# Last weight pair staged as two halves in shared float tiles, in place of four quarters in small ones

## The chip, the cores and the metric

The kernel runs on one core of one Trainium2 chip. The metric is device time in microseconds (us) of one execution; lower is better. The core has TensorE (PE) for matmuls, with its weight loads shown as a row of their own (PEld), VectorE (DVE), ScalarE (ACT), GpSimd (POOL), and SyncE (SP), which here issues all the transfers. Each engine takes its instructions strictly in the order in which the program holds them, and waits for other engines through semaphores.

## The reference, cut to what matters

An attention over 8 batches and 8 heads (576 positions, 64 dims) adds a downsampled softmax attention and a local one (distance under 4); its output is 4,608 tokens of 512 features, which go through a two-matrix feed-forward with a squared ReLU.

```
def _attn_ref(q, k, v):
    q_d = q.reshape(B, H, Sd, factor, D).mean(axis=3)   # k_d, v_d alike, factor 4
    out_up = np.repeat(sm_attn(q_d, k_d, v_d), factor, axis=2)
    mask = np.abs(pos[:, None] - pos[None, :]) < factor
    scores = np.where(mask, scale * np.matmul(q, k.transpose(0, 1, 3, 2)), -1000000000.0)
    ...
    return (out_up + np.matmul(attn, v)).astype(np.float32)

def _moe_ref(x, w_in, w_out, s, b):
    h = x @ w_in                  # (4608, 512) @ (512, 2048)
    r = np.maximum(h, 0.0)
    g = s * (r * r) + b
    return (g @ w_out).astype(np.float32)
```

The weights arrive as 64-bit floats (read as pairs of 32-bit integers), so each must be converted before use.

## The kernel before

**Feed-forward.** Tokens are worked in 18 tiles of 256 (index t), the 2,048 hidden features in 8 pairs of 128 (index p). One step (t, p) is `gemm1`, 24 matmuls of 256 columns into `ph`, then ACT's ReLU, square and cast (`gh`) and DVE's remainder (`gl`), and two or three steps later `gemm2`, 12 matmuls of 512 columns into `po`. The list `order` sets the steps: t = 0 and 1 alternate over p = 0 to 6 (steps 0 to 13), t = 2 over p = 0 to 6 (steps 14 to 20), then p = 7 for t = 0, 1, 2 (steps 21 to 23), then t = 3 onwards with all eight p.

**Weights.** `split_w(p)` makes the weights of pair p, `wi` and `wo`, as a high part (a cast on ACT) and a low part (a subtraction on DVE). `convert` does it for one chunk in seven instructions: ACT scales the top words into a float tile `es` (L226), DVE clips, shifts and twice merges bits (L227 to L230), ACT casts (L231), DVE subtracts (L234). Pairs 0 to 6 are staged whole, 1,024 columns of 64-bit words, in memory that later pairs will occupy (`STAGE`), in chunks of `CHUNK[p]` columns. The last pair, p = 7, has no such memory left: it comes in four quarters of 256 columns for each of its two matrices (`load_quarter`), in tiles with the tag `pv`, of which there are two; the quarter's `es` takes the other one. So the next quarter can be loaded only when the one before has been converted.

**Shared memory.** The single tiles `os` and `xl2` (4 KB in each partition) serve as `es` for pairs 2 to 6, then as token tile t = 2 (`split_x(2)` writes `xh` into `os` and `xl` into `xl2`), and later for outputs.

**Attention between the steps.** `advance` lets the attention of later batches go forward between the steps. `first_unit(b, hp)` is one unit: downsampled scores `sa`, local scores `sl` for the first and the second head (48 matmul records each), softmax on ACT and DVE, transposes `tp` and `tr`, then `up` and two products `ol`. Its PSUM banks come from a ring:

```
rings = {1: banks(5, 6), 2: banks(5), 3: banks(2, 3, 5)}
yield from first_unit(*units[i], rings[min(i // HP + i // (EU - 2), 3)])
```

Units (2, 0) and (2, 1) have bank 5 alone: each of their PSUM results must be read by DVE or ACT before the next can be written.

**Bias rows.** After step 13 `add_rows` sums the rows of all `wo` into `bias`, p = 7 first: 31 DVE additions of 512 columns (L577, L579), wanted only at step 21.

**What decides the order.** A scheduler puts every engine's instructions in order at build time, by priorities and a timeline of its own; the source order alone does not tell it.

Of the kernel before, what the change touches and what calls it, by code (L numbers as in the profile page):

```python
# [13 lines left out]
I32 = mybir.dt.int32  # L14
# [5 lines left out]
P = 128  # L20
# [28 lines left out]

STAGE = (6, 6, 7, 6, 7, 6, 7)  # L50
CONVERT_AT = (1, 2, 4, 6, 7, 8, 11)
CHUNK = (512, 512, 512, 1024, 1024, 512, 1024)
BEHIND = {1: 400, 2: 100, 4: 100, 5: 400}
HF = 7
GROUPS = [(i // HP, i % HP // 2) for i in range(EU, B * HP, 2)]
# [7 lines left out]
def attention_ffn_kernel(ctx, tc, qk, vw_in, vr_in, vdm, qkn, vn, w_in, w_out, s_in, b_in, out):  # L63
    nc = tc.nc
# [3 lines left out]
    one = ctx.enter_context(tc.tile_pool(name="one", bufs=1))  # L68
    two = ctx.enter_context(tc.tile_pool(name="two", bufs=2))
# [122 lines left out]
    wi, wo, wst = {}, {}, {}  # L192

    src_i = w_in.bitcast(I32).rearrange("(k c) f -> c k f", c=P)
    src_o = w_out.bitcast(I32).rearrange("(j f) c -> f j c", f=P)
# [6 lines left out]
            nc.sync.dma_start(st.rearrange("p (k f) t -> p k (f t)", k=src.shape[1]), src)  # L202
            wst[(p, op)] = st

    def load_quarter(p, op, i):
        if op == "i":
            src = src_i[:, i, 512 * p : 512 * p + 512]
        else:
            src = src_o[:, 2 * p + i // 2, 512 * (i % 2) : 512 * (i % 2) + 512]
        st = two.tile([P, 256, 2], I32, tag="pv", name="wst")  # L210
        nc.sync.dma_start(st.rearrange("p f t -> p (f t)"), src)
        return st

    def convert(st, hi, lo, op, p):


        n = hi.shape[1]
        top, low = st[:, :, 1], st[:, :, 0]
        if p in (0, 1, 7):
            f = two.tile([P, n], F32, tag="pv", name="es")  # L220
        else:
            f = one.tile([P, n], F32, tag="xl2" if op == "i" else "os", name="es")
        w = f.bitcast(I32)


        nc.scalar.mul(f, top.bitcast(F32), 2.0 ** -112)  # L226
        nc.vector.tensor_scalar(f, f, W_MAX, -W_MAX, ALU.min, ALU.max)  # L227
        nc.vector.tensor_scalar(w, w, 3, 0x7FFFFFF8, ALU.logical_shift_left, ALU.bitwise_and)
        nc.vector.scalar_tensor_tensor(w, low, 29, w, ALU.logical_shift_right, ALU.bitwise_or)
        nc.vector.scalar_tensor_tensor(w, top, -0x80000000, w, ALU.bitwise_and, ALU.bitwise_or)  # L230
        nc.scalar.copy(hi, f)  # L231
        for i in range(0, n, 512):
            js = slice(i, min(i + 512, n))
            nc.vector.tensor_tensor(lo[:, js], f[:, js], hi.bitcast(F32)[:, js], ALU.subtract)  # L234

    def split_w(p):
        with tc.high_priority(offset=-BEHIND.get(p, 0)):
            split_parts(p)

    def split_parts(p):  # L240
        wi[p] = one.tile([P, 2, NK, 256], F32R, tag=f"wi{p}", name="wi")
        wo[p] = one.tile([P, 2, 2, DM], F32R, tag=f"wo{p}", name="wo")
        for op, w in (("i", wi[p]), ("o", wo[p])):
            fl = w.rearrange("p s k f -> p s (k f)")
            if p < len(STAGE):
                st = wst.pop((p, op))
                for j in range(0, 1024, CHUNK[p]):
                    js = slice(j, j + CHUNK[p])
                    convert(st[:, js], fl[:, 0, js], fl[:, 1, js], op, p)
            else:  # L250
                for i in range(4):
                    cs = slice(256 * i, 256 * i + 256)
                    convert(load_quarter(p, op, i), fl[:, 0, cs], fl[:, 1, cs], op, p)


    xt = {}
# [513 lines left out]
```

## Time and profile before

| | us |
|---|---|
| median of 3 runs | 974.49 (971.71 to 974.57) |
| profiled execution, its own time | 972.49 |
| its span, first to last instruction | 970.7 |
| PE busy in the span | 938.7 (97%) |
| DVE, ACT, POOL busy | 637.7, 475.0, 418.0 |

Times in the trace count from the start of the span. A matmul's recorded end is modelled, so PE's busy share says that it had work, and not how fast it went; the distance from one matmul's start to the next tells that. "Idle before" a row is the engine's idle time just ahead of it, with the instruction that ended it.

### The profile page before, as it was taken

To read this page: it belongs to the slowest core of one execution; us is meant where nothing else is said; L and a number is where in the kernel's file an instruction comes from. 1 tells how busy PE (TensorE), PEld (TensorE's weight loads), DVE (VectorE), ACT (ScalarE), POOL (GpSimd) and SP (SyncE) were. 2 spreads that over 40 slices of the span, in tenths; PEclk is the share of its full clock that TensorE was granted. 3 is DMA by queue.
4 is the path that set the end of the run, shared out by engine and by line. 5 is a ranking of instruction groups with operands and counts; after the bars stand their busy time and mean duration, and the time that the engine had idled before them with its cause. 6 is when DMAs were issued, how large, how long until landed. Compare 5 with 4: busy or idle time off the path is not lost.

```text
span 970.7 us, 18541 instructions
## 1 busy us (share of the span) xinstructions
PE 938.7 (97%) x7316; PEld 843.4 (87%) x7316; DVE 637.7 (66%) x1175; ACT 475.0 (49%) x1141; POOL 418.0 (43%) x455
## 2 busy tenths in 40 slices
PE   5769999999999999999999999999999999999998
PEld 4559988888999999998888899989899999998987
DVE  5999996864567878787787878787878521211121
ACT  5878775553754453545363545453635433333231
POOL 9421011101066686776868786867676200000000
PEclk9999999999999999999999999999999999999999
DMA  9736512112243232323241424242412000000000
GB/s 316 261 121 210 172 60 78 49 42 73 101 134 113 77 110 72 102 70 133 67 136 66 135 68 131 72 134 69 136 55 76 1 22 1 23 1 22 1 23 22
DMA packets 32103, 86.26 MB, mean 89 GB/s; under 512 B 3344, under 2 KB 7952, under 8 KB 32016
## 3 DMA queue, kind: packets, MB, share of 16 engines
q1 hardware_dynamic: 32016, 85.08, 26.6%
q8 instruction: 57, 0.93, 0.4%
q14 instruction: 30, 0.25, 0.1%
HBM read 75.63 MB, written 9.44 MB: 88 GB/s over the span
## 4 chain that ended last, share of the span: by engine, by line
PE 74%; DVE 9%; DMA 8%; POOL 5%; ACT 2%; issue 2%; SPq 0%; DVEq 0%; ACTq 0%; POOLq 0%
PE ph L556 11%; PE ph L557 11%; PE ph L558 11%; PE po L603 11%; PE po L601 11%; PE po L602 11%; DMA tqk<-in_qk_dram 3%; POOL pr L466 3%; POOL acc L488 3%; DMA wst<-in_moe_w_out_dram 2%; PE sa L303 2%; DVE bias L579 1%; PE up L339 1%; PE ol L431 1%; DMA lqk<-in_qkn_dram 1%
## 5 line engine op out<-in xcount | busy, mean ns | idle before, releaser
L556 PE MATMUL ph<-xh,wi 128*128 128x256 f32 x1152 | 325.4, 283 | 3.7 <-ACT xh L542 2.5
L557 PE MATMUL ph<-xl,wi 128*128 128x256 f32 x1152 | 323.9, 281 | 0.0
L558 PE MATMUL ph<-xh,wi 128*128 128x256 f32 x1152 | 323.6, 281 | 0.0
L466 POOL TENSOR_TENSOR pr<-lqk 128x576 f32<-128x576 f32 x140 | 201.2, 1461 | 73.2 <-DMA lqk<-in_qkn_dram 29.2
L556 PEld LDWEIGHTS ph<-xh,wi 128*128 128x128 f32 x1152 | 217.5, 189 | 11.2 <-ACT xh L542 2.8
L557 PEld LDWEIGHTS ph<-xl,wi 128*128 128x128 f32 x1152 | 217.4, 189 | 5.4 <-issue 0.2
L558 PEld LDWEIGHTS ph<-xh,wi 128*128 128x128 f32 x1152 | 217.6, 189 | 0.3
L566 ACT ACTIVATE ph<-ph 128x512 f32<-128x512 f32 x144 | 83.8, 582 | 229.0 <-PE ph L558 223.2
L601 PE MATMUL po<-wo,gh 128*128 128x512 f32 x456 | 180.7, 396 | 0.0
L602 PE MATMUL po<-wo,gh 128*128 128x512 f32 x456 | 180.5, 396 | 0.0
L603 PE MATMUL po<-wo,gl 128*128 128x512 f32 x456 | 177.9, 397 | 0.0
L569 DVE TENSOR_TENSOR gl<-ph,gh 128x512 fp32r<-128x512 f32 x114 | 77.8, 683 | 115.8 <-ACT gh L568 115.5
L488 POOL TENSOR_TENSOR acc<-acc,pv 128x576 f32<-128x576 f32 x80 | 114.4, 1430 | 57.1 <-DVE acc L488 29.5
L468 DVE TENSOR_REDUCE st<-pr 128x9 f32<-128x576 f32 x140 | 105.9, 757 | 37.7 <-POOL pr L466 35.4
L292 POOL TENSOR_TENSOR dq<-vq 64x64 f32<-64x64 f32 x58 | 22.8, 393 | 197.4 <-PE up L337 195.3
L603 PEld LDWEIGHTS po<-wo,gl 128*128 128x128 f32 x456 | 85.7, 188 | 17.6 <-issue 0.2
L487 DVE TENSOR_TENSOR pv<-lv,st 128x576 f32<-128x576 f32 x120 | 87.5, 747 | 18.8 <-POOL acc L488 18.4
L601 PEld LDWEIGHTS po<-wo,gh 128*128 128x128 f32 x456 | 85.7, 188 | 15.9 <-ACT gh L568 0.6
L602 PEld LDWEIGHTS po<-wo,gh 128*128 128x128 f32 x456 | 85.7, 188 | 15.8
L568 ACT CAST gh<-ph 128x512 fp32r<-128x512 f32 x114 | 66.9, 587 | 64.3 <-PE po L602 62.4
L567 ACT ACTIVATE ph<-ph 128x512 f32<-128x512 f32 x144 | 83.7, 582 | 3.2
L602 PE MATMUL po<-wo,gb 128*128 128x512 f32 x120 | 47.1, 392 | 0.0
(149 smaller groups left out, 1239.3 us busy)
## 6 DMA issues: line engine op xcount, KB each, us to landing
tqk<-in_qk_dram SPq DMA_DIRECT2D x30, 584.0 KB, 4.1
lqk<-in_qkn_dram SPq DMA_DIRECT2D x20, 768.0 KB, 4.2
lv<-in_vn_dram SPq DMA_DIRECT2D x20, 480.0 KB, 3.4
out_dram<-os SPq DMA_DIRECT2D x17, 512.0 KB, 3.1
wst<-in_moe_w_in_dram SPq DMA_DIRECT2D x7, 1024.0 KB, 6.5
wst<-in_moe_w_out_dram SPq DMA_DIRECT2D x7, 1024.0 KB, 5.3
tvd<-in_vdm_dram SPq DMA_DIRECT2D x29, 160.0 KB, 2.9
tvr<-in_vr_dram SPq DMA_DIRECT2D x29, 128.0 KB, 3.1
```

What stands on the lines that cost most here:

```text
L466: nc.gpsimd.tensor_tensor(pr, lqk[:, 0:CH], lqk[:, CH + o : 2 * CH + o], ALU.mult)
L468: nc.vector.tensor_reduce(ls[:, :, o], pr, AX.X, ALU.add)
L487: nc.vector.tensor_tensor(pv, lv[:, o : o + CH], w, ALU.mult)
L488: (nc.vector if o % 3 == 1 else nc.gpsimd).tensor_tensor(acc[:, :, h], acc[:, :, h], pv, ALU.add)
L556: nc.tensor.matmul(ph[:, j], wi[p][:, 0, k, f], xh[:, k], start=(k == 0), stop=False)
L557: nc.tensor.matmul(ph[:, j], wi[p][:, 0, k, f], xl[:, k], start=False, stop=False)
L558: nc.tensor.matmul(ph[:, j], wi[p][:, 1, k, f], xh[:, k], start=False, stop=(k == NK - 1))
L566: nc.scalar.activation(ph, ph, AF.Relu)
L567: nc.scalar.activation(ph, ph, AF.Square)
L601: nc.tensor.matmul(po[m], gh[:, j, ms], wo[p][:, 0, j], start=first, stop=False)
L602: nc.tensor.matmul(po[m], gh[:, j, ms], wo[p][:, 1, j], start=False, stop=False)
L603: nc.tensor.matmul(po[m], gl[:, j, ms], wo[p][:, 0, j], start=False, stop=last)
```

## The change

The p = 7 weights come in two halves of 512 columns for each matrix, the first staged in `os` and the second in `xl2`, so two halves of a matrix can be in flight at once; the second matrix's halves need the same two tiles. The float tile `es` of p = 6 moves from `os` and `xl2` to the two `pv` tiles (2 KB), and so p = 6 is converted in chunks of 512 columns in place of 1,024. There are 4 loads of 512 KB in place of 8 of 256 KB, and 4 conversions in place of 8 for p = 7, 4 in place of 2 for p = 6.

```
-CHUNK = (512, 512, 512, 1024, 1024, 512, 1024)
+CHUNK = (512, 512, 512, 1024, 1024, 512, 512)
...
-    def load_quarter(p, op, i):
-        if op == "i":
-            src = src_i[:, i, 512 * p : 512 * p + 512]
-        else:
-            src = src_o[:, 2 * p + i // 2, 512 * (i % 2) : 512 * (i % 2) + 512]
-        st = two.tile([P, 256, 2], I32, tag="pv", name="wst")
-        nc.sync.dma_start(st.rearrange("p f t -> p (f t)"), src)
+    def load_half(p, op, i):
+
+        src = src_i[:, 2 * i : 2 * i + 2, 512 * p : 512 * p + 512] if op == "i" else src_o[:, 2 * p + i]
+        st = one.tile([P, 512, 2], I32, tag=("os", "xl2")[i], name="wst")
+        to = st.rearrange("p (k f) t -> p k (f t)", k=2) if op == "i" else st.rearrange("p f t -> p (f t)")
+        nc.sync.dma_start(to, src)
         return st
...
-        if p in (0, 1, 7):
+        if p in (0, 1, 6, 7):
             f = two.tile([P, n], F32, tag="pv", name="es")
...
-                for i in range(4):
-                    cs = slice(256 * i, 256 * i + 256)
-                    convert(load_quarter(p, op, i), fl[:, 0, cs], fl[:, 1, cs], op, p)
+                for i in range(2):
+                    cs = slice(512 * i, 512 * i + 512)
+                    convert(load_half(p, op, i), fl[:, 0, cs], fl[:, 1, cs], op, p)
```

The scheduler then orders three engines and SP's queue anew from step 0 to step 24; POOL's order stays as it was, and behind step 27 PE's does too. From the changed function on, the changed kernel's line numbers are one lower, so L578 there is L579 here.

SP's queue, where it issues the last quarters; before:

```order
L211 DMA wst<-in_moe_w_in_dram 128x512 x2
L114 DMA tvr<-in_vr_dram 128x256
L114 DMA tvd<-in_vdm_dram 80x512
L211 DMA wst<-in_moe_w_out_dram 128x512
L114 DMA tvw<-in_vw_dram 128x768
L211 DMA wst<-in_moe_w_out_dram 128x512 x3
L114 DMA tqk<-in_qk_dram 128x1168
```

And with the change:

```order
L210 DMA wst<-in_moe_w_in_dram 128x2x512 x2
L114 DMA tvw<-in_vw_dram 128x768
L210 DMA wst<-in_moe_w_out_dram 128x1024 x2
L114 DMA tqk<-in_qk_dram 128x1168
L114 DMA tvr<-in_vr_dram 128x256
```

The halves stand next to each other in two pairs, and one attention load (`tqk`) stands right behind the second pair. Two more quarters (of `wi`) stood further ahead in the queue before; they are gone.

DVE's queue around the first local scores `sl` of unit (2, 0), the unit with bank 5 alone, at steps 14 and 15; before, the last quarter's conversion (`es`, `wo`) stands ahead of them and among them, and the bias rows begin behind them:

```order
L230 SCALAR_TENSOR_TENSOR es<-wst,es 128x256
L393 TENSOR_REDUCE sm<-sl 128x6
L234 TENSOR_TENSOR wo<-es,wo 128x256
L394 TENSOR_TENSOR pl<-sl,sm 128x192
L577 TENSOR_TENSOR bias<-wo 128x512
L569 TENSOR_TENSOR gl<-ph,gh 128x512
```

And with the change, from the last product `ol` of the unit before, (1, 3), up to the same two readings of `sl` (here L392 and L393):

```order
L433 TENSOR_TENSOR x<-ol,ups 128x288
L578 TENSOR_TENSOR bias<-bias,wo 128x512
L542 TENSOR_TENSOR xl<-x,xh 128x4x192
L578 TENSOR_TENSOR bias<-bias,wo 128x512 x2
L303 TENSOR_REDUCE dmx<-sa 96x3
L277 TENSOR_REDUCE kd<-tqk 128x144
L578 TENSOR_TENSOR bias<-bias,wo 128x512 x2
L311 RECIPROCAL dsm<-dsm 96x3
L578 TENSOR_TENSOR bias<-bias,wo 128x512
L392 TENSOR_REDUCE sm<-sl 128x6
L578 TENSOR_TENSOR bias<-bias,wo 128x512
L393 TENSOR_TENSOR pl<-sl,sm 128x192
```

All conversions now stand ahead of this stretch, and 12 of the bias additions have moved ahead of the scores' reduction; one more stands between the two readings of `sl`.

PE's queue at the same scores; before, eight matmuls of `gemm2` stand between the first head's scores (the row with x22 ends them) and the second's:

```order
L388 MATMUL sl<-tqk 32x32 x22
L603 MATMUL po<-wo,gl 128x512
L601 MATMUL po<-wo,gh 128x512
L602 MATMUL po<-wo,gh 128x512
L603 MATMUL po<-wo,gl 128x512 x2
L601 MATMUL po<-wo,gh 128x512
L602 MATMUL po<-wo,gh 128x512
L603 MATMUL po<-wo,gl 128x512
L383 LDWEIGHTS idb
L383 MATMUL sl<-maskb,idb 128x192
L388 MATMUL sl<-tqk 32x32 x24
```

And with the change, right behind the 24 matmuls of step 14:

```order
L557 MATMUL ph<-xh,wi 128x256
L382 LDWEIGHTS idb
L382 MATMUL sl<-maskb,idb 128x192
L387 MATMUL sl<-tqk 32x32 x24
L382 LDWEIGHTS idb
L382 MATMUL sl<-maskb,idb 128x192
L387 MATMUL sl<-tqk 32x32 x24
L600 MATMUL po<-wo,gh 128x512
```

The two heads' scores follow each other directly, one step earlier than before.

## Rows read from the trace of the kernel before

**Rows 1.** The page's first part: busy time and share of each engine.
```profile
PE 938.7 (97%) x7316; PEld 843.4 (87%) x7316; DVE 637.7 (66%) x1175; ACT 475.0 (49%) x1141; POOL 418.0 (43%) x455
```
**Rows 2.** PE's waits from 75 us on: total us, times, longest.
```profile
PE sl L383 <- DVE pl L394: 1.1, 1, 1.1
PE ph L556 <- DVE gb L569: 1.0, 2, 0.6
PE ot L498 <- POOL acc L488: 1.0, 1, 1.0
PE sl L383 <- ACT pd L307: 0.5, 1, 0.5
PE ph L556 <- DVE gl L569: 0.2, 1, 0.2
```
**Rows 3.** Windows: length, busy PE, PEld, DVE, ACT, POOL, clock, DMA share, GB/s.
```profile
150.00:175.00 25.00, 24.98 (x206) 21.22 (x206) 13.41 (x33) 13.11 (x35) 2.41 (x6) 1.00 0.26 82
175.00:200.00 25.00, 23.87 (x208) 20.16 (x207) 24.15 (x44) 12.05 (x29) 4.47 (x6) 1.00 0.17 52
...
800.00:825.00 25.00, 25.00 (x169) 22.91 (x168) 3.78 (x6) 9.03 (x15) 0.00 (x0) 1.00 0.00 1
```
**Rows 4.** SP's timeline, the last quarters: start, us, instruction.
```profile
143.97 5.71 SPq L211 DMA_DIRECT2D wst<-in_moe_w_in_dram  x2
...
159.72 11.78 SPq L211 DMA_DIRECT2D wst<-in_moe_w_out_dram  x3
```
**Rows 5.** Chain of waits, 171 to 197 us: start, us, what.
```profile
171.16 2.63 DMA wst<-in_moe_w_out_dram
...
195.74 0.70 DVE bias L579
196.46 0.59 ACT ph L566
```
**Rows 6.** PE's timeline at unit (2, 0): start, us, instruction [idle before, releaser].
```profile
173.40 0.59 PE L388 MATMUL sl<-tqk 64*32 64x32 f32 x44
173.92 0.50 PE L603 MATMUL po<-wo,gl 128*128 128x512 f32 x1
...
175.65 0.39 PE L603 MATMUL po<-wo,gl 128*128 128x512 f32 x1
177.10 0.26 PE L383 MATMUL sl<-maskb,idb 128*128 128x192 bf16 x1 [1.06 <-DVE pl L394]
...
178.87 0.28 PE L556 MATMUL ph<-xh,wi 128*128 128x256 f32 x1
178.98 0.28 PE L557 MATMUL ph<-xl,wi 128*128 128x256 f32 x1
```
**Rows 7.** DVE's timeline: token tile, softmax, bits of a quarter, bias.
```profile
156.06 0.96 DVE L543 TENSOR_TENSOR xl<-x,xh 128x768 fp32r<-128x768 f32 x1 [0.20 <-ACT xh L542]
...
169.51 0.60 DVE L304 TENSOR_REDUCE dmx<-sa 96x3 f32<-96x432 f32 x1
170.03 0.74 DVE L278 TENSOR_REDUCE kd<-tqk 128x144 f32<-128x576 f32 x1
...
175.45 0.42 DVE L230 SCALAR_TENSOR_TENSOR es<-wst,es 128x256 int32<-128x256 int32 x1
175.79 0.35 DVE L393 TENSOR_REDUCE sm<-sl 128x6 f32<-128x192 f32 x1
...
176.69 0.35 DVE L394 TENSOR_TENSOR pl<-sl,sm 128x192 f32<-128x192 f32 x1
...
178.16 0.68 DVE L579 TENSOR_TENSOR bias<-bias,wo 128x512 f32<-128x512 f32 x1
```
**Rows 8.** DVE's timeline at 51 us: the same merge on 512 columns.
```profile
51.80 0.68 DVE L229 SCALAR_TENSOR_TENSOR es<-wst,es 128x512 int32<-128x512 int32 x1
```
**Rows 9.** A later unit's scores, on PE, and their first reader on DVE.
```profile
226.88 0.62 PE L388 MATMUL sl<-tqk 64*32 64x32 f32 x48
227.87 0.34 DVE L393 TENSOR_REDUCE sm<-sl 128x6 f32<-128x192 f32 x1
```
**Rows 10.** DMA issues, weights: count, KB each, median us to landing.
```profile
wst<-in_moe_w_out_dram SPq DMA_DIRECT2D x7, 1024.0 KB, 5.3
...
wst<-in_moe_w_out_dram SPq DMA_DIRECT2D x4, 256.0 KB, 2.7
```

## The prediction

> **What bounds the kernel now.** I read the page's busy shares first: PE is busy 938.7 us of the 970.7 us span, DVE two thirds, ACT half, POOL less [rows 1]. So the question is where PE waits. PE's waits from 75 us on, when the first weights are ready, are five rows with 3.8 us in all [rows 2]. Two are of one kind: the scores `sl` (L383) wait 1.1 us for DVE's L394 and 0.5 us for ACT's L307. Both belong to units (2, 0) and (2, 1), which have PSUM bank 5 alone. The rest (gb, acc and gl, 2.2 us) the change does not touch. What PE does in its busy time the edit leaves as it is: the same matmuls on the same operands.
>
> Next I read what the edit is about. In SP's timeline the second matrix's quarters are issued in a row of three that takes 11.78 us, and the last two of the first matrix take 5.71 us [rows 4]: each waits until the one before is converted, since the two `pv` tiles hold one quarter and its `es`. The chain of waits goes through these loads (one of 2.63 us at 171 us), then through DVE's bias additions, and from there through an ACT row to PE [rows 5]. This looks as if the loads set the time. They don't. The chain follows ACT's and DVE's own queues backward, and PE was busy nearly all that time: 24.98 us of 25 from 150 to 175 us, and 23.87 from 175 to 200 [rows 3]. DVE on the other hand is busy only 13.41 us from 150 to 175; its idle 11.6 us are the waits for quarters. That is what bigger halves remove, and it lies beside PE's work.
>
> **The change part by part.**
>
> *Instructions.* A merge of bits on 256 columns shows 0.42 us [rows 7], on 512 columns 0.68 [rows 8]; so the part that does not shrink with the columns is 2 x 0.42 - 0.68 = 0.16 us. For p = 7, four conversions in place of eight save 4 x 5 = 20 DVE instructions, 3.2 us; p = 6 gets two more conversions, and each matrix's merges come in two pieces, so I count 2 x 5 = 10 at most, +1.6 us. DVE gains about 1.6 us, ACT (two instructions a conversion, 8 fewer, 4 more) under 1 us. On PE's time I put this at nothing: PE's own work covers it, as from 150 to 175 us [rows 3]. Without this cover the most it could give is the 1.6 us.
>
> *Loads.* A quarter lands 2.7 us after its issue, a load of 1,024 KB 5.3 us [rows 10]. A half of 512 KB lies between; on a straight line it takes 3.6 us, my estimate. Eight serial rounds become four in two overlapping pairs. The second pair waits in SP's queue for the first matrix's conversion, and behind it stand `tqk`, `tvr` and `tvd` of the next units. PE waits for none of these loads from 75 us on [rows 2], and their users come later in PE's queue. I take zero; a loss has its bound in the slower rival below.
>
> The Trainium skill ("DMA: Bandwidth & Descriptors", section "Anatomy of one DMA — SWDGE (gpsimd) path") gives, for a queue of another kind than SP's here, a fixed cost of about 2 us per transfer and a term by bytes; by it I estimate 2.6 us for a quarter and 3.2 us for a half, so eight serial quarters cost 21 us and four halves 13 us. Its advice to batch transfers speaks for a gain of 8 us. The trace agrees on the quarter (2.7 us), but not that PE waits for it.
>
> *Memory.* `os` and `xl2` now hold the halves until they are converted, and only then may `split_x(2)` write token tile t = 2 into them. Before, its `xl` began at 156.06 us and took 0.96 us [rows 7], while nothing else wanted the tiles. Now `xl` stands behind all conversions in DVE's queue. Its first user, step 14, stands behind 12 matmuls of `gemm2` and the scores `sa`. This is the tight place, priced as a rival.
>
> *The scores of unit (2, 0).* This is where PE's order changes for the worse. Before, eight matmuls of `gemm2` stand between the heads' scores; their starts run from 173.92 to 175.65, seven steps of 0.25 us, and then PE still waits 1.06 us for L394 [rows 6]. In the changed order the second head's scores come directly behind the first's, in the same bank. PE then waits for the whole round: from the scores' end to DVE's first reader at most 0.37 us (226.88 + 0.62 to 227.87, with DVE still busy before [rows 9]), L393 0.27, one bias addition 0.60, L394 0.35 [rows 7], and 0.06 from L394's end to PE's start (177.04 to 177.10 [rows 6, 7]). A row's time overlaps the next start by 0.08 (169.51 + 0.60 against 170.03), which is taken off L393 and the addition. Sum 1.65 us in place of 1.06: +0.6. If DVE reads at once and the addition slips behind, it is 0.7 us, so -0.4.
>
> *The scores of unit (2, 1).* Their wait of 0.5 us [rows 2] should go, since more than 30 feed-forward matmuls now stand between the last `sa` and the next `sl`: at 0.11 us for one of `gemm1` (178.87 to 178.98 [rows 6]) over 3 us. -0.5; at the other end it stays, 0.
>
> *Switches.* Where a `gemm2` follows attention matmuls, it shows 0.50 us and not 0.39 [rows 6]. In steps 2 to 27 I count 90 borders between the two kinds in place of 86: 4 x 0.11 = +0.4, between 0 and that.
>
> *Sum.* 0.6 - 0.5 + 0.4 = +0.5 us. With the bounds the sum runs from -0.9 to +1.0. The profiled execution took 972.49 us, 2.0 below the median of 974.49; the difference is worked on the execution's rows and added to the median: 975.0.
>
> **The rivals.**
>
> *Slower: DVE comes late to bank 5.* From the last `ol` of unit (1, 3) to the first scores of unit (2, 0), PE now has 12 matmuls of 0.25, `sa`, 24 of 0.11 and the scores of 0.62: 6.3 us and `sa` besides [rows 6, 9]. DVE has in that stretch a sum into `x` (like L394, 0.35), six bias additions of 0.60, `xl` 0.96, L304 0.52 and L278 0.66 [rows 7]: 6.1 us, with small rows besides. So the margin is some tenths, and from there each us that DVE is late costs PE one. It is late if the last half's conversion ends after that `ol`. A half's round is 3.6 us of load, an ACT scaling, and four DVE rows of 0.60 [rows 8, 10]: 6.5 us, of which 2.4 lie beside the other half's conversion. All of the rest exposed, 4.1 us, gives 974.5 + 0.5 + 4.1 = 979. Against it: the 11.6 us of idle time that DVE sheds ahead of this place [rows 3] are more than the 7.2 us of 12 bias additions moved there. For it: four more conversions' worth of work cannot start before SP's queue lets the second pair go.
>
> *Faster: the loads set the time after all.* If the chain of waits is right [rows 5], eight rounds of 2.7 become four of 3.6 [rows 10]: 21.6 - 14.4 = 7 us at most. What speaks for a part of it is that the weight loads' row is less full here than later: 21.22 and 20.16 us in these two windows, against 22.91 in a stretch of plain feed-forward [rows 3]. If that gap is hidden waiting, it holds 2 x 22.91 - 41.4 = 4.4 us, and the time would be 974.5 - 4.4 = 970. [...] Against it: attention matmuls are small, so another mix of them fills that row less without any wait, and the waits that the trace names there are 1.6 us [rows 2].
>
> *It doesn't do what it says.* If the second pair of halves is held by the first matrix's conversion so long that DVE is idle as before, the bias rows stay where they were in time, and PE's waits too. Within the measurement: 974.5.
>
> **How the numbers follow.** A measurement of this kernel tells about 0.3%, 2.9 us, from no change. My forecast, PE-bound and within tenths of a per cent, gets 0.70; the unchanged time 0.06, which is the same case by its time; slower by DVE 0.13; faster 0.11. Of the forecast's cases all are within 0.3% but for the spread of runs (971.71 to 974.57 before), for which I take 0.02 off and give it to both sides. So faster 0.12, same 0.74, slower 0.14; the prediction is 975.0. The range of 971.0 to 978.5 takes in the bounds of the sum, that spread, and half of each rival's span; what is left out is the far part of the two rivals.
>
> **What the profile after would show.** Right: PE's wait at the scores of unit (2, 0) of 1.4 to 1.8 us, for DVE's L393 (its number after), and none for ACT's pd at unit (2, 1); four `wst` issues of 512 KB landing in 3 to 4 us, the last before 160 us; DVE's idle time from 150 to 175 us under 4 us; PE's waits from 75 us still under 5 us. Wrong: a wait of PE's for `xh` or `xl` at step 14, or for `sl` of over 2 us, says that DVE is late (slower). A shorter span from 150 to 225 us with the same count of matmuls and the same waits would say that PE's busy time held hidden waiting (faster). A wait for `tqk` or `tvr` would say that SP's queue is blocked by the halves.

## The result

| | us |
|---|---|
| kernel before, median of 15 runs | 972.11 (970.62 to 974.57) |
| changed kernel, median of 15 runs | 975.82 (972.75 to 978.94) |
| ratio, 95% interval | 1.0037 (1.0024 to 1.0050) |
| profiled execution of the changed kernel, its own time | 972.75 |

The change makes the kernel slower by about 0.4%, 3.6 us by the ratio. The 975.0 us of the prediction lie close to the measured median, but that is partly luck: the three runs shown of before had a high median, 974.49, and over 15 runs it is 972.11. What the prediction said of the difference, +0.5 us, is too small, and 0.37% is just over the 0.3% that it took for no change. The profiled execution of the changed kernel is the fastest of its 15; single executions can't be compared here.

The page's first part for the changed kernel, against [rows 1]:

```profile
PE 937.1 (97%) x7316; PEld 841.0 (87%) x7316; DVE 636.8 (66%) x1163; ACT 474.6 (49%) x1137; POOL 420.8 (43%) x455
```

The same 7,316 matmul records, 12 DVE instructions fewer. TensorE's waits from 75 us on, against [rows 2]; line numbers are one lower, as in the order:

```profile
PE sl L382 <- DVE pl L393: 1.3, 1, 1.3
PE ot L497 <- POOL acc L487: 0.5, 1, 0.5
PE ph L555 <- DVE gb L568: 0.5, 1, 0.5
PE po L600 <- ACT gh L567: 0.4, 1, 0.4
```

They sum to 2.7 us, where before had 3.8. So the waits didn't get longer, and no row here says where 3.6 us went. Windows of 150 to 200 us, against [rows 3]:

```profile
150.00:175.00 25.00, 23.68 (x256) 20.89 (x255) 23.75 (x44) 13.24 (x34) 3.92 (x6) 1.00 0.17 53
175.00:200.00 25.00, 25.00 (x209) 20.93 (x208) 15.77 (x29) 13.05 (x33) 3.60 (x6) 1.00 0.10 29
```

DVE's idle time from 150 to 175 us is 1.25 us, not 11.6: the change does what it says. The halves on SP's queue, against [rows 4], and in the list of DMA issues (KB each, median us to landing), against [rows 10]:

```profile
126.27 4.54 SPq L210 DMA_DIRECT2D wst<-in_moe_w_in_dram  x2
143.03 0.94 SPq L210 DMA_DIRECT2D wst<-in_moe_w_out_dram  x2
```

```profile
wst<-in_moe_w_in_dram SPq DMA_DIRECT2D x2, 512.0 KB, 3.6
wst<-in_moe_w_out_dram SPq DMA_DIRECT2D x2, 512.0 KB, 4.0
```

The last half is issued at 144 us, where the last quarter was issued at 171 us. The Trainium skill ("DMA: Bandwidth & Descriptors", section "Anatomy of one DMA — SWDGE (gpsimd) path") gave 3.2 us for a half by my estimate, for a queue of another kind than SP's; the trace shows 3.6 and 4.0. The gain of 8 us that its advice on larger transfers would give here is refuted: the loads ended 27 us sooner, and the kernel got slower.

**Where the time went.** TensorE has the same work from the first matmul of step 2 to the first of step 28, and behind step 27 its order is the same. I took both starts from each trace: 176.2 us in the kernel before, 178.6 in the changed one, +2.4. Here the changed kernel's TensorE works on the second head's scores of unit (2, 1), at step 19:

```profile
202.56 0.26 PE L382 MATMUL sl<-maskb,idb 128*128 128x192 bf16 x1
202.74 0.38 PE L387 MATMUL sl<-tqk 64*32 64x32 f32 x20
203.05 0.39 PE L556 MATMUL ph<-xl,wi 128*128 128x256 f32 x1
203.37 0.24 PE L387 MATMUL sl<-tqk 64*32 64x32 f32 x2
203.54 0.38 PE L557 MATMUL ph<-xh,wi 128*128 128x256 f32 x1
203.86 0.25 PE L387 MATMUL sl<-tqk 64*32 64x32 f32 x2
...
205.33 0.38 PE L387 MATMUL sl<-tqk 64*32 64x32 f32 x20
205.64 0.50 PE L602 MATMUL po<-wo,gl 128*128 128x512 f32 x1
```

Five single matmuls of `gemm1` are put between the scores' matmuls. And the same scores in the kernel before:

```profile
205.73 0.26 PE L383 MATMUL sl<-maskb,idb 128*128 128x192 bf16 x1
205.92 0.62 PE L388 MATMUL sl<-tqk 64*32 64x32 f32 x48
206.47 0.51 PE L603 MATMUL po<-wo,gl 128*128 128x512 f32 x1
```

The reader is to subtract starts. Whole, the scores take 206.47 - 205.73 = 0.74 us. In pieces they take 205.64 - 202.56 = 3.08; less five `gemm1` matmuls of 0.12 that is 2.48, so the five breaks cost 1.74 us, 0.35 each. One of them by itself: from 203.37 to 203.86 are 0.49 us for a `gemm1` matmul of 0.12 and two of the 48 scores' matmuls. No idle time stands beside any of these rows: TensorE counts as busy.

A product `ol` of unit (2, 0) is cut three times in the same way; first the changed kernel, then a whole product of the kernel before:

```profile
187.82 0.38 PE L430 MATMUL ol<-db,tvw 128*64 128x96 f32 x2
188.13 0.39 PE L555 MATMUL ph<-xh,wi 128*128 128x256 f32 x1
...
189.70 0.54 PE L430 MATMUL ol<-db,tvw 128*64 128x96 f32 x6
190.17 0.50 PE L602 MATMUL po<-wo,gl 128*128 128x512 f32 x1
```

```profile
190.18 0.72 PE L431 MATMUL ol<-db,tvw 128*64 128x96 f32 x12
190.82 0.50 PE L601 MATMUL po<-wo,gh 128*128 128x512 f32 x1
```

That is 2.35 us, less three `gemm1` matmuls 2.0, against 0.64: +1.35 us. The kernel before had three such breaks, in the first head's scores of unit (2, 0):

```profile
171.97 0.26 PE L383 MATMUL sl<-maskb,idb 128*128 128x192 bf16 x1
172.01 0.36 PE L558 MATMUL ph<-xh,wi 128*128 128x256 f32 x1
172.21 0.28 PE L556 MATMUL ph<-xh,wi 128*128 128x256 f32 x1
172.42 0.24 PE L388 MATMUL sl<-tqk 64*32 64x32 f32 x2
172.59 0.38 PE L557 MATMUL ph<-xl,wi 128*128 128x256 f32 x1
172.91 0.24 PE L388 MATMUL sl<-tqk 64*32 64x32 f32 x2
173.08 0.38 PE L558 MATMUL ph<-xh,wi 128*128 128x256 f32 x1
```

Up to the next `gemm2` at 173.92 us [rows 6] this is 1.95 us, less four `gemm1` matmuls 1.47, against 0.74: +0.7 us. In the changed order these scores are whole.

### The profile page after: what moved, and what is told of

Same layout as the page of the kernel before. It is cut to its first block, busy times and chain, and to the rows that moved or that the text cites. A ratio compares the mean times of both kernels' runs of the same rounds, so it can differ in the third digit from the quotient of the medians.

```text
span 971.0 us, 18506 instructions
## 1 busy us (share of the span) xinstructions
PE 937.1 (97%) x7316; PEld 841.0 (87%) x7316; DVE 636.8 (66%) x1163; ACT 474.6 (49%) x1137; POOL 420.8 (43%) x455
## 4 chain that ended last, share of the span: by engine, by line
PE 84%; DVE 6%; POOL 5%; DMA 2%; issue 1%; ACT 1%; DVEq 0%; POOLq 0%
PE ph L555 13%; PE ph L556 13%; PE ph L557 13%; PE po L600 13%; PE po L602 12%; PE po L601 12%; PE sa L302 2%; POOL pr L465 2%; POOL acc L487 2%; DMA tqk<-in_qk_dram 1%; PE ol L430 1%; PE up L338 1%; PE ot L497 1%; DMA lqk<-in_qkn_dram 1%; PE sl L387 1%
```

## The experiments

The first theory after the result: **breaks**, eight in place of three, explain it. Its rivals: the **clock**, since the mean granted clock of the first profile was 0.981 and before it was 1.000; and **DVE late** or the halves' loads and memory.

**1 and 2. Both kernels again,** without an edit.

> The changed kernel once more, to see how firm the 0.4% is and what the granted clock does. All three theories expect a ratio to the kernel before near 1.0037 (1.0024 to 1.0050). Breaks theory (TensorE pays 0.35 to 0.5 us each time one feed-forward matmul is put inside a unit's scores or products): the same order, so again eight breaks and about +2.4 us between steps 2 and 28, whatever the clock. Clock theory: its granted clock is below that of the kernel before by the same 1 to 2 points as the first time.

> The kernel before as a candidate, so that its granted clock is listed run by run. Ratio 1.000 within 0.15%. Clock theory: all its runs show a clock of 0.995 or more, while those of the changed kernel show 0.98 to 0.99. Breaks theory and late-DVE theory: its clock is sometimes 0.98 too, and its time does not follow the clock.

Measured: the changed kernel 1.0040 (1.0026 to 1.0054), the kernel before 1.0004 (0.9995 to 1.0014). Steps 2 to 28 took 178.7 and 176.4 us, so in these two kernels the stretch repeats within 0.2 us, closer than the whole time does. The clock theory falls: 28 executions of the kernel before had clocks from 0.979 to 1.000 as well (971.23 us at 1.000, 970.50 at 0.979), and the second profile of the changed kernel is at 1.000 and no faster (974.77 us). Where the clock falls early, it is in the first 75 us. The changed kernel's first profile:

```profile
25.00:50.00 25.00, 18.19 (x304) 15.11 (x305) 24.61 (x59) 21.65 (x62) 9.35 (x11) 0.59 0.70 246
50.00:75.00 25.00, 16.06 (x201) 13.40 (x201) 24.76 (x52) 18.08 (x41) 5.99 (x7) 0.66 0.41 137
```

DVE is busy 24.6 and 24.8 us of 25 there, and TensorE, for part of these windows at half its clock (1.2 GHz), still waits. Step 2 starts no later for the fall: at 78.7 us with it, and without it at 80.8 us in the second trace of the changed kernel and at 79.9 in the kernel before.

**3 and 4. Scores and products of batch 2 kept together,** in either kernel:

```
+    def whole(b):
+        return tc.high_priority() if b == 2 else contextlib.nullcontext()
...
-            for g in range(NG):
+            with whole(b):
+                for g in range(NG):     # likewise around the matmuls of ol
```

> The changed kernel with the matmuls of one head's scores and of one product kept together for batch 2 (higher scheduling priority), nothing else in the source. Its TensorE order has no broken scores or products. Breaks theory: the 3.1 us that the eight breaks cost (1.8 in one scores tile, 1.35 in one product) come back: ratio 1.0005, between 0.999 and 1.002. Late-DVE theory (bank 5 and the conversions): no change, 1.0037. Clock theory: no change, 1.0037, with a clock of 0.98.

> The kernel before with the same addition. It had three breaks in one scores tile, about 0.7 us over an unbroken one. Breaks theory: ratio 0.9993, between 0.998 and 1.000. The other two theories: 1.000.

Measured: 1.0035 (1.0021 to 1.0050) and 1.0075 (1.0057 to 1.0093). Taken by ratio, breaks are refuted, and no theory expected the second. The traces say why these ratios don't decide it: in the first, steps 2 to 28 took 176.2 us, 2.4 less than in the changed kernel, but the priority also reordered the program behind step 28, and there it lost time again: the waits for POOL's `acc` and for `gb` are 3.6 us, where they were 1.0. In the second the waits grew in both parts (a `po` for `gh` three times, 1.2 us in all, and 5.7 us for `acc`, `gb` and `gl` behind 245 us). An edit that reorders more than it means to is no test.

**5, 6 and 11. The two broken groups alone kept together,** with the condition narrowed (`whole` takes it as its argument):

```
+            with whole(b == 2 and hp == 1 and h == 1):    # scores
+            with whole(b == 2 and hp == 0 and f == 1):    # product ol
```

Experiment 5 has both lines, 6 only the second, 11 only the first.

> The changed kernel, where only the two broken groups are kept together: the product ol of unit (2, 0), second half, and the scores of unit (2, 1), second head. TensorE's order differs from the changed kernel's in 18 places of steps 17 to 19, DVE's and ACT's in 5 and 4, nothing behind step 20. Breaks theory: eight breaks fewer, 3.1 us less in steps 17 to 19 by the trace of the changed kernel, so a ratio of 1.0005 (0.9995 to 1.0015). Rival (the rest of the new order, or the late half of the program, is what costs): 1.003 to 1.004, as the changed kernel.

> As before this, but the product ol alone is kept together: TensorE's order differs from the changed kernel's in 10 places, no other engine's differs. Breaks theory: three breaks fewer, 1.35 us, so a ratio of 1.0023 (1.001 to 1.0035). Rival: no change, 1.0037.

> The changed kernel with the scores of unit (2, 1), second head, kept together and the product ol left in its four pieces. Breaks theory: 1.76 us less for five breaks, about 0.4 us of it given back at the transposes behind them as in the run with both groups whole: ratio 1.0022 (1.001 to 1.0035), steps 2 to 28 in 177.2 us. Rival: no change, 1.0037 and 178.65 us.

Measured: 1.0011 (0.9996 to 1.0025) with both, 1.0014 (1.0000 to 1.0028) with `ol` alone, 1.0026 (1.0012 to 1.0040) with the scores alone. All three are within what the breaks theory expected, though the third doesn't exclude its rival, 1.0037. The first, whose estimate lies below the whole interval of the changed kernel, takes back some seven tenths of the loss. Steps 2 to 28 took 176.2 us with both, as in the kernel before. With one alone they took 178.25 and 179.4, more than expected, and these two traces show something new. Experiment 6 behind the scores of unit (2, 0), first windows, then TensorE's rows:

```profile
170.00:172.00 2.00, 0.68 (x54) 0.47 (x45) 1.88 (x5) 1.97 (x6) 0.00 (x0) 1.00 0.00 0
172.00:174.00 2.00, 2.00 (x53) 1.68 (x53) 1.84 (x5) 0.43 (x1) 0.00 (x0) 0.69 0.31 53
174.00:176.00 2.00, 2.00 (x10) 1.90 (x10) 2.00 (x6) 0.52 (x1) 0.00 (x0) 0.50 0.64 248
```

```profile
171.76 0.26 PE L386 MATMUL sl<-maskb,idb 128*128 128x192 bf16 x1 [1.32 <-DVE pl L397]
...
172.88 0.63 PE L606 MATMUL po<-wo,gh 128*128 128x512 f32 x1
173.31 0.63 PE L605 MATMUL po<-wo,gh 128*128 128x512 f32 x1
```

TensorE had been busy 0.68 of 2 us, and then the granted clock fell from 1.00 to 0.50, from 2.4 to 1.2 GHz; the next `po` matmuls start 0.43 us apart and not 0.23. Over the stretch this cost 1.4 us (the excess of the feed-forward matmuls among their like over 0.1175 us for `gemm1` and 0.230 for `gemm2` is 2.2 us, and 0.8 without a fall). Less this, experiment 6 has 176.85 us, 1.8 less than the changed kernel, where its rows gave 1.35 for the breaks of `ol`. Its edit did a little more than its name says: the scores of unit (2, 1) have four breaks in its trace and not five, another 0.35 us. Experiment 11 has the same fall, and a wait of 0.7 us for `gl` that is new; less 1.4 us for the fall and 0.8 us of waits more, it has 177.2 us, as expected. A fall in this stretch stands in four of the 13 traces: behind a pause of 1.3 us (experiments 6 and 11), of 1.5 (8), and behind two of 1.3 and 0.7 (4). It stands in neither trace of the kernel before, whose longest pauses there are 1.1 and 1.0 us.

**7, 8 and 13. Either part of the change alone.** The halves with p = 6 as before (7, and 13 again; this edit of the changed kernel), and p = 6 in chunks of 512 with the quarters (8; the reverse edit, in the kernel before):

```
-CHUNK = (512, 512, 512, 1024, 1024, 512, 512)
+CHUNK = (512, 512, 512, 1024, 1024, 512, 1024)
-        if p in (0, 1, 6, 7):
+        if p in (0, 1, 7):
```

> The halves without the other part: p = 6 keeps its float tiles in os and xl2 and chunks of 1,024. One broken group, a short sa, in place of the one scores tile with three breaks before. Breaks theory: 0.7 us less for these breaks, so a ratio near 0.9995 (0.998 to 1.001). Rival (the halves in os and xl2 hold up the token tile, or their loads hold up others in SP's queue): 1.002 to 1.004, with a TensorE wait for xh or xl at step 14.

> The quarters stay; only p = 6 goes to chunks of 512 in the small tiles. Its TensorE order has eight breaks (two scores tiles cut once, one tr cut once, one scores tile cut five times), three before. Breaks theory: five more at 0.35 us, 1.7 us, so a ratio of 1.0018 (1.0005 to 1.003). Rival (only the halves cost): 1.000.

> The halves without the part for p = 6, once more and on the same chip as the run with the heads apart. Breaks and wait theory: its order has neither, so again 0.9976 (0.9966 to 0.9990) and steps 2 to 28 in 173.8 us. Rival (the first result was the chip's luck): 1.000.

Measured: the halves alone are faster than before, 0.9976 (0.9966 to 0.9987) and again 0.9972 (0.9960 to 0.9984), with steps 2 to 28 in 173.75 and 175.2 us; p = 6 alone is slower, 1.0036 (1.0020 to 1.0051), with 179.8 us, of which one more fall of the clock and 0.6 us more of waits hold a part. Experiments 7 and 8 miss the ranges of the breaks theory, one on either side. So the halves, which the change is named for, gain 2.3 to 2.7 us, and the chunks of p = 6 lose 3.5; the two don't add, since together they are at 3.6. DVE's share doesn't tell the versions apart: from 150 to 175 us DVE is busy 24.45 us in experiment 7 and 23.75 in the changed kernel, and one is faster than before, the other slower. TensorE's order differs with each. That of the halves alone has one break, in a short `sa`, and the heads' scores of unit (2, 0) stand far apart (waits of 0.3 us in the stretch of experiment 7, 1.3 in that of 13); that of p = 6 alone has eight breaks.

**12. The two heads of unit (2, 0) apart,** in the changed kernel:

```
+    def behind():
+        return tc.issue_after(getattr(sent[-1], "ins", sent[-1]))   # last gemm2 matmul
...
+            with behind() if (b, hp, h) == (2, 0, 1) else contextlib.nullcontext():
```

> The changed kernel with one constraint on the order: the second head's scores of unit (2, 0) are issued after the gemm2 matmuls that precede them in the source. In TensorE's queue eight gemm2 matmuls then stand between the two heads, and, as the order turns out, no scores or products are broken any more; behind step 23 nothing differs from the changed kernel. Breaks and wait theory: 2.45 us less for the breaks and at least 0.9 of the 1.3 us of the wait, so steps 2 to 28 in 175.0 to 175.5 us and a ratio of 0.9985 (0.997 to 1.0005). Rival (only breaks count, the pause is hidden): 1.0011 as with the two groups whole. Rival (the loads or the memory of the halves cost): no better than 1.0011.

Measured: 1.0010 (0.9994 to 1.0025), steps 2 to 28 in 176.2 us: the first rival. (The traced execution, 970.06 us, is the fastest of twelve with a median of 974.36; what the slower ones lose, its trace can't show.) The breaks are gone, the wait for DVE is gone, and TensorE waits at the same place for something else, longer:

```profile
170.61 0.50 PE L607 MATMUL po<-wo,gh 128*128 128x512 f32 x1 [2.04 <-ACT gh L574]
```

and ACT's rows ahead of it:

```profile
168.45 1.01 ACT L319 ACTIVATE pd<-pd,dsm 96x144 f32<-96x144 f32 x3
169.37 0.58 ACT L573 ACTIVATE ph<-ph 128x512 f32<-128x512 f32 x1
169.98 0.59 ACT L574 CAST gh<-ph 128x512 fp32r<-128x512 f32 x1
```

ACT's square stands behind three scalings of the softmax, and `gemm2` needs its cast. In the changed kernel this lay beneath the wait for `sl`. There the cast ends at 170.49 us, and `gemm2` starts at 170.56, as ACT's timeline and TensorE's show:

```profile
169.90 0.59 ACT L567 CAST gh<-ph 128x512 fp32r<-128x512 f32 x1
170.56 0.50 PE L600 MATMUL po<-wo,gh 128*128 128x512 f32 x1
```

So taking the wait for `sl` away gives back nothing at this place. Experiments 9 and 10, which were to take it away by putting both heads' scores in one bank, gave no result: nothing in them orders the two heads' writes to that bank.

## Why the prediction was right, and where it was not

*What bounds the kernel* held in the main: the loads ended 27 us sooner and DVE lost its idle time, and the changed kernel is no faster. The faster rival, the chain of waits taken at its word with its 7 us, is refuted. But that the loads lie beside PE's work was too plain a reading. The last quarter of the kernel before lands at 173.79 us [rows 5], and ACT and DVE wait for it:

```profile
173.87 0.43 ACT L226 ACTIVATE es<-wst 128x256 f32<-128x256 f32 x1 [0.41 <-DMA wst<-in_moe_w_out_dram]
174.33 0.29 DVE L227 TENSOR_SCALAR es<-es 128x256 f32<-128x256 f32 x1 [1.93 <-ACT es L226]
```

DVE's L227 to L230 of this quarter stand ahead of L393, which so reads the scores 1.8 us after their end (173.99 to 175.79 us): PE's wait of 1.06 us hung on a load. Experiments 7 and 13 have no such wait; their waits in the stretch are 0.3 and 1.3 us against 1.8 before. So of what the halves gain, a part may be the loads' and the rest is TensorE's order; no run separates the two.

*Instructions, loads, memory* held for the changed kernel: no wait for `xh`, `xl`, `tqk` or `tvr` appears, a half lands in 3.6 to 4.0 us against an estimate of 3.6. The slower rival, DVE late at bank 5, didn't happen: DVE arrives in time, as the changed kernel's timelines show, DVE's and then TensorE's.

```profile
168.54 0.36 DVE L392 TENSOR_REDUCE sm<-sl 128x6 f32<-128x192 f32 x1
168.81 0.68 DVE L578 TENSOR_TENSOR bias<-bias,wo 128x512 f32<-128x512 f32 x1
169.41 0.35 DVE L393 TENSOR_TENSOR pl<-sl,sm 128x192 f32<-128x192 f32 x1
```

```profile
167.87 0.62 PE L387 MATMUL sl<-tqk 64*32 64x32 f32 x48
169.82 0.26 PE L382 MATMUL sl<-maskb,idb 128*128 128x192 bf16 x1 [1.32 <-DVE pl L393]
```

*The scores of unit (2, 0)* waited 1.32 us, where I said 1.65 and bounds of 0.7 and 1.65: the addition does stand between, and only the way from TensorE to DVE was too long (0.05 us, from 168.49 to 168.54). *The scores of unit (2, 1)* lost their wait of 0.5 us, as said; another of 0.4 us came, for `gh`. The waits of the stretch together are 1.75 us before and 1.69 after.

*Switches* is the step that failed. The count of 90 borders in place of 86 is right, but the price of 0.11 us for each, and with it the bound of 0.4 us for the sum, is not: the stretch, less its waits, grew by 2.46 us. A border's price isn't one number: a feed-forward matmul inside a group of scores costs 0.35 us over its own time, one inside a product 0.45. A group of scores with the three transposes `tp` put among its matmuls (143.56 to 145.36 us in the changed kernel) costs 0.8 more than the two apart, while both products of a unit in a row give back 0.35; with smaller differences these two come to about nothing. The count of borders hid all this, since breaks added borders and joins took others away. The prices were to be had from the kernel before, which has three such breaks at 172 us; I read that piece of the timeline for its wait and not for the distances of its starts.

*The size.* The range of 971.0 to 978.5 us was drawn wide for the spread of the runs and for two rivals that did not come, and it held a loss of another cause; that is luck as well. Of the 3.6 us, 2.4 are in the stretch in both traces of the changed kernel, by the rows 1.75 + 1.35 for its eight breaks less 0.7 for the three of before, and experiment 5, which mends the eight, takes 2.4 back. About 1 us, no more than the half-width of the ratio's interval, stays open. The falls of the clock, 1.4 us in two of the six traces whose order has both heads' scores in a row, would give half of it; that is argued from six traces, not shown.

## What to carry to other kernels

When a scheduler reorders the program, compare TensorE's queue before and after for small groups that are cut by single matmuls of another shape, and price a cut by the distances between starts: it stands in no idle time and no wait. Judge an edit by a stretch with the same work, from one matmul to another; here it repeats within 0.2 us in two kernels and 1.4 in a third, where whole executions of one kernel spread by 4 to 7 us. And try the parts of a change alone: the halves without the chunks for p = 6 are the version that beats both kernels, at 0.9972 to 0.9976 of the time before.

## What the runs showed of the hardware

A break costs more than the two borders of 0.11 us that it adds to the count: around one `gemm1` matmul between scores (203.37 to 203.86 us) 0.17 us pass before it and 0.32 from its start to the next scores, against 0.12 for a matmul among its like. And the granted clock fell to half, 1.2 GHz, for some 3 us in four of 13 traces, behind pauses of TensorE of 1.3 us (experiments 6 and 11), 1.5 (8), and 1.3 and 0.7 (4), while a pause of 2.0 us in experiment 12 and of 1.3 us in four other traces left it at 1.00.
